# Attention in blocks of 64 tokens on 64x64 tiles of the array: the front of an attention and mixer kernel, before and after

## The chip, the cores and the metric

The kernel runs on one core of a Trainium2 chip. The metric is the device time of one execution in microseconds (us). Each kernel was run several times (the kernel before: 698.68 to 700.90 us over all rounds). One execution of each kernel is recorded by the hardware profiler, and the views below are of that execution; its time can differ by a few tenths of a per cent from the median.

Names of engines in the views: PE is TensorE (matrix products), PEld its weight loads, DVE is VectorE, ACT is ScalarE, POOL is GpSimd, SP is SyncE, which here issues DMA.

Some words: PSUM is the memory that TensorE writes its results to, and a bank is one of its parts. "Tile" has three meanings here: the 128 tokens of one step, a part of TensorE's array that works on a product of its own (as in "four tiles share a round"), and a named buffer (as in "a PSUM tile"). A record is one instruction in the trace; a float32 product of the attention is two matmul records, each with a weight load (the eight products of pkv in a step are 16 records, and the page of the kernel before counts 4194 matmuls and 4194 loads). A round is one start on each of the tiles of the array in use.

## The reference

Part one is attention with decay, in blocks of 64 tokens, with a running 64x64 state for each batch and head. Part two is a token mixer of low rank followed by a channel MLP.

```python
# q, k, v: (4, 8, 768, 64) float32; lam: (8,)
for b in range(nb):                       # 12 blocks of 64 tokens
    sl = slice(b * block, (b + 1) * block)
    qb, kb, vb = (q[:, :, sl], k[:, :, sl], v[:, :, sl])
    intra = np.einsum('bhic,bhjc->bhij', qb, kb) * Dmask[None]
    intra = np.einsum('bhij,bhjd->bhid', intra, vb)
    inter = np.einsum('bhid,bhde->bhie', qb * lam_pow[None], kv_state)
    out[:, :, sl] = intra + inter
    rev_pow = lam[:, None, None] ** (block - 1 - pos[None, :, None])
    kb_dec = kb * rev_pow[None]
    kv_state = lam_block[None, :, None, None] * kv_state + np.einsum('bhsd,bhse->bhde', kb_dec, vb)
...
# x = out as (4, 768, 512); U (768, 32), V (32, 768)
h = x.transpose(0, 2, 1) @ U @ V
u = x + h.transpose(0, 2, 1)
ch = np.maximum(u @ w_ch1, 0.0) @ w_ch2   # 512 -> 2048 -> 512, the weights come as float64
return (u + ch).astype(np.float32)
```

## The kernel before

The kernel first runs the attention (the "front"), and then the two big products of the MLP, which take about 540 us and which the change does not touch. The front goes over 24 tiles of 128 tokens, six for each batch, and one such tile is called a step below. The kernel before treats a tile as one block of 128 tokens. A pair of heads shares the 128 partitions (P = 128, D = 64, HP = 4 pairs, CT = 4).

```python
def prep(s):                                   # q and k with the head dimension on partitions
    ...
    for name, dst in (("q", qt), ("k", kt)):
        pt = bank([P, n, P], "p" + name, "b2") # a PSUM bank each for q and for k
        for a in range(a0, a0 + n):
            nc.tensor.transpose(out=pt[:, a - a0, :], in_=raw[s, name][:, 2 * a : 2 * a + 2, :],
                                identity=ident)
        nc.scalar.copy(dst[:, a0 : a0 + n, :], pt)

def scores(s):                                 # two row tiles, 64x128
    pss = [bank([P, HP, P], "pss", "a1") for x in range(2)]
    for a in range(HP):
        for x in range(2):
            rows = slice(x * D, (x + 1) * D)
            nc.tensor.matmul(out=pss[x][:, a, :], lhsT=kt[rows, a, :], rhs=qt[rows, a, :],
                             start=True, stop=True)
    ...                                        # sm = pss * mask, VectorE

def outputs(s):                                # two column tiles, 128x64; x comes transposed
    px = bank([P, HP, P], "px", "a2")
    for a in range(HP):
        if c > 0:
            for x in range(2):
                rows = slice(x * D, (x + 1) * D)
                nc.tensor.matmul(out=px[rows, a, :], lhsT=kv[:, a, rows], rhs=qs[:, a, :],
                                 start=True, stop=False)
        for x in range(2):
            nc.tensor.matmul(out=px[x * D : (x + 1) * D, a, :], lhsT=vr[:, 2 * a + x, :],
                             rhs=sm[:, x, a, :], start=(c == 0), stop=True)
    nc.scalar.copy(xt, px)
    ...                                        # state(s): pkv products, the state in kv,
                                               # a block-diagonal matrix padded with zeros

def back(s):                                   # x back to tokens on partitions
    for ct in range(CT):
        nc.tensor.transpose(out=px[:, ct, :], in_=xt[:, ct, :], identity=ident)
    nc.scalar.copy(xs[s].rearrange("p (c n) -> p c n", n=P), px)

# one step in program order (cut):
# prep(s+1), turned, scale(s+1), mix, [low at a batch border], outputs(s),
# [low_sum at a border], scores(s+1), back(s), turn
```

In these names `mix` adds the mixer's result to x (product pu), `turn` transposes x for the big products (put), and `turned` is the rest of that splitting on ScalarE and GpSimd. `low` and `low_sum` are the products of low rank, needed once for each batch ("border").

## Time and profile before

| | |
|---|---|
| time, median of 3 | 700.32 us (699.53 to 700.9) |
| front: start to the first matmul of the big products (pz) | 142.2 us |
| the rest | 555.3 us |
| TensorE busy over the span | 98% |
| one steady step of the front | 5.67 us |
| TensorE matmul records in a steady step | 81 |

The prediction below shows the main views of this profile. Two more are needed for the comparison. The first is from the page of the kernel before: the busy tenths of TensorE in 40 equal slices of the span (17.4 us each), and the line of the DMA queue that carries instructions (packets, MB, share).

### The profile page before, as it was taken

Reading aid. Unit: us, or ns where it says so; the run is one execution under the profiler, and the core shown is the slowest. Engines: PE = TensorE matmul, PEld = TensorE weight load, DVE = VectorE, ACT = ScalarE, POOL = GpSimd, SP = SyncE. Lnnn points to the kernel's source line nnn. Section 1 sums busy time; section 2 is a strip of 40 time slices with the busy share of each in tenths; the row PEclk is TensorE's granted clock in tenths of the full one; section 3 lists DMA queues with packets and bytes.
Section 4 is the critical chain, followed back from the end, with each engine's and each line's share of the span. In section 5 each row is a group of like instructions: output and inputs, shape, how many; then the busy total and the mean of one; then the engine's idle time right before and its main releaser. Section 6 shows DMA issues by size and latency. Waiting matters only on the chain.

```text
span 697.5 us, 11418 instructions
## 1 busy us (share of the span) xinstructions
PE 685.6 (98%) x4194; PEld 556.0 (80%) x4194; DVE 502.0 (72%) x905; ACT 306.6 (44%) x543; POOL 108.0 (15%) x91
## 2 busy tenths in 40 slices
PE   7999999998999999999999999999999999999997
PEld 6879797976888888888888888888888888888886
DVE  5768687867899777777779436778577586775864
ACT  4767777844566544444455322232232222322320
POOL 4425554523000000000000000011030030300300
PEclk9999999999999999999999999999999999999999
DMA  9977686224476565556557889966344363352521
GB/s 219 228 182 183 167 221 163 90 81 168 173 256 245 197 210 210 208 209 208 205 206 266 296 304 359 341 206 200 98 153 155 91 211 103 120 185 91 166 92 60
DMA packets 131530, 131.17 MB, mean 188 GB/s; under 512 B 81234, under 2 KB 89426, under 8 KB 131474
## 3 DMA queue, kind: packets, MB, share of 16 engines
q1 hardware_dynamic: 129376, 129.92, 57.8%
q10 hardware_dynamic: 2098, 0.52, 0.3%
q8 instruction: 33, 0.54, 0.3%
q14 instruction: 23, 0.19, 0.1%
HBM read 80.09 MB, written 50.33 MB: 187 GB/s over the span
## 4 chain that ended last, share of the span: by engine, by line
PE 93%; DVE 4%; issue 1%; ACT 1%; DMA 1%; ACTq 0%; DVEq 0%
PE pz L638 25%; PE pz L771 13%; PE pz L769 13%; PE pd L773 13%; PE pd L648 12%; PE pss L341 3%; PE px L364 3%; PE px L359 2%; PE pxn L404 2%; PE pkv L380 2%; PE put L464 1%; PE pk L306 1%; PE pq L306 1%; DVE ut L469 1%; DVE sm L347 1%; PE pr L433 1%
## 5 line engine op out<-in xcount | busy, mean ns | idle before, releaser
L638 PE MATMUL pz<-u_hl,w 128*128 128x512 f32 x768 | 190.6, 398 | 1.1 <-ACT uf L476 1.1
L638 PEld LDWEIGHTS pz<-u_hl,w 128*128 128x128 f32 x768 | 144.4, 188 | 37.1 <-ACT uf L476 1.5
L771 PE MATMUL pz<-w_hl,m 128*128 128x512 f32 x384 | 151.6, 396 | 0.0
L769 PE MATMUL pz<-w_hl,m 128*128 128x512 f32 x384 | 151.6, 396 | 0.0
L773 PE MATMUL pd<-w_d,m 128*128 128x512 f32 x384 | 150.0, 396 | 0.0
L752 ACT ACTIVATE m<-mt 128x512 fp32r<-128x512 f32 x96 | 60.7, 632 | 196.8 <-PE pd L773 137.0
L753 DVE SCALAR_TENSOR_TENSOR m<-rm,m 128x512 fp32r<-128x512 f32 x96 | 71.5, 746 | 52.3 <-ACT m L752 52.1
L653 DVE SCALAR_TENSOR_TENSOR r<-pd,r 128x512 f32<-128x512 f32 x96 | 61.8, 686 | 57.2 <-ACT r L644 47.2
L793 POOL TENSOR_TENSOR o<-o,u 128x512 f32<-128x512 f32 x20 | 29.8, 1522 | 452.1 <-DVE o L791 452.1
L648 PE MATMUL pd<-u_d,w 128*128 128x512 f32 x384 | 98.8, 397 | 0.0
L769 PEld LDWEIGHTS pz<-w_hl,m 128*128 128x128 f32 x384 | 72.3, 188 | 17.7
L771 PEld LDWEIGHTS pz<-w_hl,m 128*128 128x128 f32 x384 | 72.3, 188 | 17.6
L773 PEld LDWEIGHTS pd<-w_d,m 128*128 128x128 f32 x384 | 72.3, 188 | 17.6
L648 PEld LDWEIGHTS pd<-u_d,w 128*128 128x128 f32 x384 | 72.2, 188 | 17.4
L644 ACT ACTIVATE r<-pz 128x512 f32<-128x512 f32 x96 | 51.9, 593 | 62.4 <-PE pz L638 62.4
L754 DVE SCALAR_TENSOR_TENSOR m<-m 128x512 fp32r<-128x512 f32 x96 | 69.1, 721 | 0.9
L751 DVE TENSOR_SCALAR mt<-rm 128x512 uint32<-128x512 uint32 x96 | 46.2, 482 | 28.2 <-DMA rm<-r_d 27.6
L347 DVE TENSOR_TENSOR sm<-pss,mask 128x512 f32<-128x512 f32 x48 | 30.9, 686 | 11.5 <-PE pss L341 9.3
L179 ACT CAST w<-wt 128x512 fp32r<-128x512 f32 x32 | 19.9, 622 | 41.8 <-DVE wt L176 33.5
L364 PE MATMUL px<-sm,vraw 128*64 128x128 f32 x384 | 35.4, 274 | 0.4 <-DVE x_nat L450 0.3
L359 PE MATMUL px<-qs,kv 128*64 128x128 f32 x320 | 32.1, 279 | 0.0
L136 ACT ACTIVATE sc<-sc,ends 128x512 f32<-128x512 uint32 x29 | 21.0, 723 | 19.2 <-DVE sc L132 19.2
(88 smaller groups left out, 761.9 us busy)
## 6 DMA issues: line engine op xcount, KB each, us to landing
r_d<-r SPq DMA_DIRECT2D x96, 256.0 KB, 2.7
rm<-r_d SPq DMA_DIRECT2D x96, 256.0 KB, 2.6
words<-in_moe_w_ch_dram SPq DMA_DIRECT2D x32, 512.0 KB, 4.4
w_d<-w SPq DMA_DIRECT2D x16, 768.0 KB, 3.3
w_hl<-w_d SPq DMA_DIRECT2D x16, 512.0 KB, 6.0
u_d<-x_nat SPq DMA_DIRECT2D x24, 256.0 KB, 3.0
u<-u_d SPq DMA_DIRECT2D x24, 256.0 KB, 4.3
out_dram<-o SPq DMA_DIRECT2D x24, 256.0 KB, 2.0
```

The costliest lines, as they stand in the source:

```text
L364: nc.tensor.matmul(out=px[x * D : (x + 1) * D, a, :], lhsT=vr[:, 2 * a + x, :], rhs=sm[:, x, a, :], start=(c == 0), stop=True,)
L638: nc.tensor.matmul(out=acc[g][0], lhsT=w[:, n, ct, :], rhs=uhl[g][:, n, ct, :], start=(ct == 0 and n == 0), stop=(ct == CT - 1 and n == 1),)
L644: nc.scalar.mul(rs[g], acc[g][0], 1.0 + E)
L648: nc.tensor.matmul(out=acc[g][1], lhsT=w[:, 2, ct, :], rhs=ud[g][:, ct, :], start=(ct == 0), stop=(ct == CT - 1),)
L653: nc.vector.scalar_tensor_tensor(rs[g], acc[g][1], 4096.0, rs[g], ALU.mult, ALU.add)
L751: nc.vector.tensor_scalar(t.bitcast(U32), r.bitcast(U32), HI, None, ALU.bitwise_and)
L752: nc.scalar.activation(out=m[:, 0], in_=t, func=AF.Relu)
L753: nc.vector.scalar_tensor_tensor(m[:, 1], r, 0.0, hi, ALU.max, ALU.subtract)
L754: nc.vector.scalar_tensor_tensor(m[:, 2], hi, E, low, ALU.mult, ALU.subtract)
L769: nc.tensor.matmul(out=pz, lhsT=m[:, 0, cols], rhs=hl[:, 0], start=first, stop=False)
L771: nc.tensor.matmul(out=pz, lhsT=m[:, 1, cols], rhs=hl[:, 1], start=False, stop=end)
L773: nc.tensor.matmul(out=pd, lhsT=m[:, 2, cols], rhs=dd, start=first, stop=end)
```

## The change

The intent: work in blocks of 64 tokens, as the reference does, so that all attention products are 64x64 by 64 columns. The hope is that the array then runs four of them side by side, where before two ran (pairs 7 ns apart in the single records of the trace before). The products come out with tokens on partitions, so the four transposes that turned x back go away, and the state needs no zero blocks. The number of matmul instructions doubles. The diff, cut to its core:

```diff
+    psf = front_ctx.enter_context(tc.tile_pool(name="psf", bufs=1, space=bass.MemoryType.PSUM))
+    def two_banks(name, tag):
+        return psf.tile([P, 2, N], FP32, tag=tag, name=name)
 ...
     def prep(s):
 ...
-            for name, dst in (("q", qt), ("k", kt)):
-                pt = bank([P, n, P], "p" + name, "b2")
+            both = two_banks("pqk", "qk" if a0 == 0 else "px")
+            for i, (name, dst) in enumerate((("q", qt), ("k", kt))):
+                pt = both[:, i, 0 : n * P].rearrange("p (a t) -> p a t", t=P)
 ...
+    def ahead_of(s):              # state products and scores, all on four tiles
+        both = two_banks("psk", "sk")
 ...
+        for a in range(HP):
+            for x in range(2):
+                for t in blocks:
+                    nc.tensor.matmul(out=pkv[half[x], t, a, :], lhsT=ks[half[t], a, x, :],
+                                     rhs=vr[half[t], 2 * a + x, :], start=True, stop=True)
+        for a in range(HP):
+            for t in range(2):
+                for x in range(2):
+                    nc.tensor.matmul(out=pss[half[t], x, a, :], lhsT=kt[half[x], a, half[t]],
+                                     rhs=qt[half[x], a, half[t]], start=True, stop=True)
 ...                               # states kvb (after the first block), kva (after the second)
+    def inter(s):                 # queries x state, four tiles
+        st[s]["px"] = both = two_banks("px", "px")
 ...
+                            out=px[half[t], x, a, :], lhsT=st[s]["qs"][half[x], a, t, :],
+                            rhs=kv[s][half[x], a, :], start=(a == 0), stop=False)
+        st[s]["seen"] = nc.scalar.copy(...)      # one element: orders the two row groups
+    def intra(s):                 # scores x values, two diagonal tiles
 ...
+                        out=px[half[t], x, a, :], lhsT=sm[half[t], x, a, :],
+                        rhs=vr[half[t], 2 * a + x, :], ...)
+        nc.scalar.copy(xs[s].rearrange("p (a x e) -> p x a e", a=HP, x=2), px)
-    def back(s):                  # the four transposes of x: gone
 ...
-        pp = bank([P, C], "pp", "a2" if b < B - 1 else "b2")
+        pp = two_banks("pp", "px")[:, 0] if b < B - 1 else bank([P, C], "pp", "b2")
 ...
-        step = [("prep", s + 1)] * (s + 1 < NS)
+        step = [("prep", s + 1), ("fade", s + 1)] * (s + 1 < NS)
+        step += [("mix", done)] * (done >= 0)
+        step += [("low", b - 1)] * (c == 0 and b > 0)
+        step += [("inter", s)]
         step += [("turned", done - 1)] * (done > 0)
         step += [("scale", s + 1)] * (s + 1 < NS)
         step += [("aside", s)]
-        step += [("mix", done)] * (done >= 0)
-        step += [("low", b - 1)] * (c == 0 and b > 0)
-        step += [("outputs", s)]
+        step += [("ahead_of", s + 1)] * (s + 1 < NS)
         step += [("low_sum", b - 1)] * (c == 0 and b > 0)
-        step += [("scores", s + 1), ("back", s)] * (s + 1 < NS)
+        step += [("intra", s)]
         step += [("turn", done)] * (done >= 0 and done // TG < FG)
```

## The prediction

Item 4's 0.4 us is the author's estimate, and what the trace before shows for it is the pass from one group to the next, 0.15 us from pkv to pss (60.25 to 60.40) and 0.20 from pss to pxn (61.29 to 61.49). The 29 ns of the first rival are half of the 58 ns from pair to pair in pkv. The 0.2 us for "seen", the copy of one element in the diff, is an estimate too: ScalarE's copies of 256 and 512 columns took 0.37 and 0.59 us in the trace before, which would leave some 0.15 for a very short one.

> **What bounds the kernel now.** I read first the page's list of engines and the chain that ended last. TensorE is busy 98% and is 93% of the chain, so the time is the length of TensorE's stream.
>
> ```profile
> PE 685.6 (98%) x4194; PEld 556.0 (80%) x4194; DVE 502.0 (72%) x905; ACT 306.6 (44%) x543; POOL 108.0 (15%) x91
> PE 93%; DVE 4%; issue 1%; ACT 1%; DMA 1%; ACTq 0%; DVEq 0%
> ```
>
> The change touches only the attention front, so next I cut the span into stretches. The timeline shows the first matmul of the two big products (pz) at 142.2 us and the last block transpose at 167.8 us.
>
> ```profile
> core 0: us, PE busy (x) PEld busy (x) DVE busy (x) ACT busy (x) POOL busy (x), PEclk, DMA share, GB/s
> 0.00:142.20 142.20, 136.89 (x1831) 117.31 (x1832) 104.66 (x229) 101.40 (x194) 66.86 (x63) 1.00 0.72 178
> 142.20:170.70 28.50, 25.73 (x135) 18.63 (x133) 20.17 (x34) 14.71 (x26) 10.03 (x8) 1.00 0.35 127
> 170.70:697.50 526.80, 522.94 (x2231) 420.09 (x2231) 377.13 (x644) 190.47 (x324) 31.13 (x21) 1.00 0.56 194
> ```
>
> The front is 142.2 us, and TensorE is its bound too (136.9 us busy; the rest is mostly the first 7 us). The last 526.8 us can't change: same matmuls, 99% busy. Third, the timeline of TensorE for one repeating step (54.11 to 59.78, 59.78 to 65.46: 5.67 us each, one tile of 128 tokens); the columns are start, duration, engine, line, operation and count. Durations overlap, so I read differences of starts.
>
> ```profile
> 59.79 0.69 PE L380 MATMUL pkv<-vraw,ks 128*64 128x64 f32 x16
> 60.40 1.16 PE L341 MATMUL pss<-qt,kt 64*128 64x128 f32 x16
> 61.49 0.66 PE L404 MATMUL pxn<-ident,xt 128*128 128x128 f32 x4
> 61.98 0.60 PE L464 MATMUL put<-ident,x_nat 128*128 128x128 f32 x4
> 62.42 0.60 PE L306 MATMUL pq<-ident,qraw 128*128 128x128 f32 x4
> 62.86 0.60 PE L306 MATMUL pk<-ident,kraw 128*128 128x128 f32 x4
> 63.21 0.48 PE L447 MATMUL pu<-vp 128*128 128x512 f32 x1
> 63.62 0.44 PE L359 MATMUL px<-qs,kv 128*64 128x128 f32 x4
> ...
> 65.46 0.34 PE L380 MATMUL pkv<-vraw,ks 128*64 128x64 f32 x4
> ```
>
> Costs from starts: pkv 0.61, pss 1.09, pxn 0.49, put 0.44, q and k 0.79, pu 0.41, px 1.84 (32 records: state part and score part); sum 5.67 us. Every fp32 product is two records. In the single records pkv goes in pairs, one on each column half, 7 ns apart, a pair every 58 ns; pss in pairs (two row halves) every 111 ns; px in pairs every 109 ns; a transpose takes 109 ns. Passing from one group to the next costs 0.15 to 0.2 us. So now two tiles of the array run together, never four.
>
> The same table for the step from 59.78 to 65.45 gives the other engines: VectorE 4.63 us, ScalarE 4.21, DMA share 0.74 (4.2 us). They are not far behind TensorE's 5.67.
>
> [...]
>
> **The change part by part** (one steady step).
> 1. Products. Four kinds, each 16 matmuls of 64x64 by 64 columns = 32 records: state x queries, keys x values, scores, scores x values. That is 128 records, where there were 64. The first three go round four different tiles: if four tiles share the 58 ns round, 8 rounds x 58 = 0.47 us each, 1.40 in all. The last uses only the two diagonal tiles: 16 rounds x 58 = 0.93. Sum 2.33 us, against pkv + pss + px = 3.54. Four records in 58 ns is 15 ns each; two stand 7 ns apart now, so four fit.
> 2. Removed: 4 transposes (pxn), 0.49 us; x comes out with tokens on partitions.
> 3. Unchanged: q, k transposes 8 x 0.109 = 0.87, put 0.44, pu 0.41.
> 4. [...]small waits between groups; I take 0.4 us.
> Sum for TensorE: 2.33 + 0.87 + 0.44 + 0.41 + 0.4 = **4.45 us**, in place of 5.67.
> 5. VectorE: one mask product of 512 fewer (0.65), one sum of 128x256 more (0.35 to 0.42): 4.63 - 0.28 = **4.35 us**. The four 64-wide updates stay.
> 6. ScalarE: xt copy (0.59) and two kv copies (0.83) go; four 64-wide scalings (my estimate 0.7 us, from the 0.53 us step of a 512-wide activation) and "seen" (0.2) come: 4.21 - 0.5 = **3.7 us**.
> 7. GpSimd: the same multiplications (1.3 + 1.07 + 1.28 us), **3.7 us**.
> 8. DMA: the same bytes in less time. The packet records have 73,728 packets of 256 bytes for q, k, v, 18 ns each: 3072 x 18 / 16 engines = 3.46 us for each tile; the u_d store 128 x 85 / 16 = 0.68. **4.1 us**, more where weights are fetched (1.66 us for 512 KB). All of the front's packets take 102.5 us of sixteen engines.
>
> So TensorE stays the bound by a hair, and four engines stand within 20% of it. Small waits won't all hide: I take **4.65 us** for a steady step, a saving of 1.0.
>
> In the first seven steps (no put, no pu; now 4.91 us each) TensorE would need 3.65, but the loads arrive each 3.46 us plus 0.6 for the U, V and w1 words. The page shows DMA at 97% from 20 to 40 us already:
>
> ```profile
> 20.00:40.00 20.00, 19.61 (x292) 17.35 (x292) 13.95 (x32) 14.52 (x30) 8.17 (x7) 1.00 0.97 233
> ```
>
> I take 4.0 us, a saving of 0.9. At batch borders the low-rank products (1.9 us more) stay.
>
> Sum over 24 steps: start 7.3; six steps at 4.0 = 24.0; first border 5.6; three steps after borders 4.9 = 14.7; nine steady at 4.65 = 41.9; two batch ends at 4.4 = 8.8; two later borders at 6.3 = 12.6; the last 3.4. Total 118.3 us against 142.2: 24 us saved. From 142 to 170 us one transpose group and one pu leave (about 1 us), but that stretch has waits on ScalarE copies that may take it back. 700.3 - 25 = 675 us.
>
> **Rivals.**
> - *Four tiles don't share a round*[...]. Then 128 x 29 = 3.7 us for the products, and a step is 5.8: no gain in steady steps, total 695 to 703. Against it: the 7 ns pairs in both column and row form[...].
> - *A half-way rate*, 20 ns for each record: 0.5 us more a step, total 685.
> - *VectorE, ScalarE or the chain between them becomes the bound*: q and k copies, then the scalings, then "seen", then the second half of the last product; in VectorE the state sum waits for the scalings. By my hand layout of a step "seen" comes about when TensorE needs it. If it doesn't, 0.3 us a step, 7 us: 682.
> - *DMA becomes the bound*: 102.5 us of work in a 118 us front[...], with buffers three or four deep. Stalls of 5 us in all are likely in the first third; they are partly in my 4.0.
> - *All better*: steady steps at 4.4 and early ones at 3.8 give 668.
>
> **Range and chances.** Centre 675, 80% range 667 to 689. Only the first rival ends within 2% (above 686.3) for sure, and I give it and bad mixes of the others about 14%. Slower by 2% would need more than 14 us of new waits in 142: 2%. Faster 0.84.
>
> **What would show it.** In the profile after: single records of the score and state products in rounds of four every 58 to 62 ns, the last product in pairs; no pxn; steady steps of 4.5 to 4.8 us; the first pz matmul near 118 us; DMA share over 0.85 in the front, and TensorE idle behind q or k loads in the first 35 us; VectorE near 90% in the steady steps. Wrong, if [...]TensorE waits on ScalarE ("seen", kt) in each step, or if the stretch after the front grows.

## More of the kernel before

```profile
PE   7999999998999999999999999999999999999997
...
q8 instruction: 33, 0.54, 0.3%
```

TensorE is nearly full from the second slice to the last, and 33 packets of 16 KB brought instructions.

## The result, and the profile after

The changed kernel takes **722.49 us** (median of 4, 721.24 to 723.83) against 699.92 us before (median of 4, 699.47 to 700.9), and its result is correct. It is slower by 3.2%: the ratio is 1.0321, with a 95% interval from 1.0297 to 1.0345. Ratios in this document are the mean time of one kernel's runs over the mean of the other's of the same rounds, so they are not quite the ratios of the medians. Executions over 1.5% slower than the fastest of the same kernel are left out of the means.

The page of the changed kernel, in the same parts as before: engines, TensorE in 40 slices of 18 us, the granted clock and the DMA share in the same slices, the instruction queue, and the chain that ended last.

```profile
PE 672.2 (93%) x5634; PEld 538.2 (75%) x5634; DVE 498.4 (69%) x918; ACT 299.8 (42%) x583; POOL 114.4 (16%) x98
...
PE   6768876789899999999999999999999999999997
...
PEclk9999999998999999999999999999999999999999
...
DMA  9956765411547666555656699985335353353421
...
q8 instruction: 44, 0.72, 0.4%
...
PE 87%; issue 5%; POOL 3%; DVE 2%; ACT 2%; DMA 1%; SPq 0%; ACTq 0%; POOLq 0%; DVEq 0%
```

TensorE has less to do (672.2 us busy, 13.4 less than before) although its matmul records went from 4194 to 5634. But it is no longer full: its first nine slices are at 6 to 8 tenths, where before all but the first were at 9. In the chain, "issue" has grown from 1% to 5%; that is time in which TensorE waited for nothing that the profile shows. The instruction queue carried 44 packets in place of 33: TensorE's matmul records and weight loads together (2 x 5634 and 2 x 4194) are 44.0 and 32.8 times 256. The loads of data are not the main cause: the DMA share falls to 0.5 to 0.7 in the third to seventh slice, and TensorE's waits for DMA in the front add up to 4.8 us, 2.0 of them at the start.

The busy time by stretch, cut as in the prediction (columns as there); the first pz matmul is now at 164.3 us and the last block transpose at 191.7:

```profile
0.00:164.30 164.30, 122.10 (x3274) 98.42 (x3274) 102.62 (x245) 95.36 (x235) 74.28 (x70) 0.95 0.63 157
164.30:191.70 27.40, 25.73 (x125) 18.80 (x125) 16.95 (x26) 11.96 (x22) 8.09 (x7) 0.93 0.26 97
191.70:721.40 529.70, 524.34 (x2239) 420.94 (x2236) 378.84 (x647) 192.43 (x328) 32.05 (x22) 1.00 0.57 194
```

The front is 22.1 us longer (164.3 against 142.2), although TensorE is busy 14.8 us less in it (122.1 against 136.9). The rest is 557.1 us against 555.3. So the loss is idle time in the front: 42 us idle, where before there were 5. The granted clock of the front is 0.95, where before it was 1.00.

Where in the front is it lost? Measured from the scores of one step to the scores of the next, a steady step without an instruction stop (shown below) takes 5.0 to 5.9 us, about as long as before (5.67) and longer than the 4.65 predicted; one with a stop takes up to 7.0. The three border steps and the steps after them take 52.3 us in place of 39.8, so they hold 12.5 of the 22.1 us.

Now TensorE's timeline for one steady step of the changed kernel (columns as in the prediction; in brackets the idle time before a group and what ended it):

```profile
69.57 0.65 PE L387 MATMUL psk<-qt,kt 64*64 64x64 f32 x32
70.04 1.11 PE L436 MATMUL px<-vraw,sm 64*64 64x64 f32 x32
71.08 0.66 PE L505 MATMUL put<-ident,x_nat 128*128 128x128 f32 x4
71.58 0.60 PE L330 MATMUL pqk<-ident,qraw 128*128 128x128 f32 x4
72.91 0.66 PE L330 MATMUL pqk<-ident,kraw 128*128 128x128 f32 x4 [0.73 <-ACT qt L334]
73.32 0.48 PE L488 MATMUL pu<-vp 128*128 128x512 f32 x1
```

The products are about as fast as predicted: the scores take 0.47 us from start to start (69.57 to 70.04; predicted 0.47) and scores x values 1.04 (predicted 0.93). But the transposes of k wait 0.73 us for ScalarE's copy of q. In the kernel before the q and k transposes ran on without a stop. The next view, TensorE's waits in the front (us in total, times, longest us), shows that this happens in every step, and that "issue" comes second:

```profile
PE pqk L330 <- ACT qt L334: 21.0, 23, 2.4
PE px L436 <- issue: 8.3, 5, 2.6
```

A look at single records answers the prediction's main question: do four tiles share a round? These are starts of the state x queries product in the same step:

```profile
68.15 0.22 PE L418 MATMUL px<-kva,qs 64*64 64x64 f32 x1
68.16 0.22 PE L418 MATMUL px<-kvb,qs 64*64 64x64 f32 x1
...
68.21 0.22 PE L418 MATMUL px<-kva,qs 64*64 64x64 f32 x1
```

Four records start within 0.02 us (68.15, 68.16, 68.16, 68.17), and the next round starts at 68.21, about 58 ns later. They do share it. So the 15 ns a record of the prediction are real, in bursts.

An issue stop looks like this in the timeline of the changed kernel. Nothing is waited for, and the product is cut in the middle of its 32 records:

```profile
27.07 0.98 PE L436 MATMUL px<-vraw,sm 64*64 64x64 f32 x26
29.73 0.39 PE L436 MATMUL px<-vraw,sm 64*64 64x64 f32 x6 [1.68 <-issue]
```

Two theories came out of this. **Theory A:** q and k share one PSUM tile of two banks, so k's transposes wait for the copy of q in the other bank; this is the larger part, about 21 us. **Theory B:** the rest are stops in the supply of instructions. A matmul of float32 is two records, each with a weight load, so a steady step has 141 records = 282 TensorE instructions in place of 162. The rival to both was that TensorE, VectorE, ScalarE and GpSimd hold each other in a ring in every step, as the prediction's third rival says, and then taking one wait away would only uncover the next.

### The profile page after: what moved, and what is told of

Its sections match the earlier page's. It is cut to its first block, busy times and chain, and to the rows that moved or that the text cites. A ratio compares the mean times of both kernels' runs of the same rounds, so it can differ in the third digit from the quotient of the medians.

```text
span 721.4 us, 14364 instructions
## 1 busy us (share of the span) xinstructions
PE 672.2 (93%) x5634; PEld 538.2 (75%) x5634; DVE 498.4 (69%) x918; ACT 299.8 (42%) x583; POOL 114.4 (16%) x98
## 4 chain that ended last, share of the span: by engine, by line
PE 87%; issue 5%; POOL 3%; DVE 2%; ACT 2%; DMA 1%; SPq 0%; ACTq 0%; POOLq 0%; DVEq 0%
PE pz L686 24%; PE pz L817 12%; PE pz L819 12%; PE pd L821 12%; PE pd L696 12%; PE px L436 3%; PE pqk L330 2%; POOL qs L353 2%; PE px L418 2%; PE psk L380 1%; PE psk L387 1%; PE put L505 1%; ACT qt L334 1%; POOL ks L342 1%; DMA kraw<-in_k_dram 1%
## 5 line engine op out<-in xcount | busy, mean ns | idle before, releaser
L800 ACT ACTIVATE m<-mt 128x512 fp32r<-128x512 f32 x96 | 60.7, 632 | 195.4 <-PE pd L821 144.1
L330 PE MATMUL pqk<-ident,kraw 128*128 128x128 f32 x96 | 17.6, 308 | 22.9 <-ACT qt L334 21.0
L436 PE MATMUL px<-vraw,sm 64*64 64x64 f32 x768 | 29.0, 222 | 8.3 <-issue 8.3
L436 PEld LDWEIGHTS px<-vraw,sm 64*64 64x64 f32 x768 | 26.1, 138 | 11.2 <-issue 11.2
L353 POOL TENSOR_TENSOR qs<-qt,powq 128x512 f32<-128x512 f32 (+1 forms) x24 | 29.0, 1209 | 29.6 <-ACT qt L334 25.0
```

The costliest lines, as they stand in the source:

```text
L436: mm = nc.tensor.matmul(out=px[half[t], x, a, :], lhsT=sm[half[t], x, a, :], rhs=vr[half[t], 2 * a + x, :], start=(c == 0 and t == 0), sto ...
L800: nc.scalar.activation(out=m[:, 0], in_=t, func=AF.Relu)
```

## The experiments

Eleven kernels ran in twelve runs; the same kernel ran twice as e5_scale_first and e5_again. e4_bench and e11_bench_wide are not in the table: they carry extra work and ran once each (757.92 and 783.35 us). Differences are against the changed kernel where nothing else is said. "Front" is the time of the first pz matmul in the profiled execution.

| run | what it is | median us | ratio to before (95%) | front us |
|---|---|---|---|---|
| before | | 699.92 | 1 | 142.2 |
| after | | 722.49 | 1.0321 (1.0297 to 1.0345) | 164.3 |
| e1_qk_apart | q and k in a PSUM tile each | 701.62 | 1.0036 (1.0019 to 1.0052) | 144.1 |
| e2_border | batch border reordered | 715.86 | 1.0233 (1.0207 to 1.0259) | 158.4 |
| e3_both | e1 and e2 | 701.05 | 1.0025 (1.0002 to 1.0049) | 146.2 |
| e5_scale_first | e1, scalings of q earlier on GpSimd | 700.26 (three fast runs) | 1.0014 (0.9998 to 1.0031) | 142.5 (e5_again) |
| e6_border2 | e5 and the border of e2 | 697.01 | 0.9965 (0.9946 to 0.9983) | 141.3 |
| e7_shift64 | e5 and 64 more instructions at the start | 703.92 | 1.0060 (1.0042 to 1.0077) | 147.7 |
| e9_spread | e6, q transposes moved into the middle | 697.64 | 0.9981 (0.9968 to 0.9995) | 137.9 |
| e10_turn_mid | e6, x transposes moved into the middle | 697.89 | 0.9981 (0.9967 to 0.9994) | 140.1 |
| e12_one_pass | e6 with bf16 in two products (less exact) | 684.59 | 0.9794 (0.9760 to 0.9828) | 126.2 |

### e1_qk_apart: the shared PSUM tile (theory A)

```diff
-            both = two_banks("pqk", "qk" if a0 == 0 else "px")
+            both = None if a0 == 0 else two_banks("pqk", "px")
             for i, (name, dst) in enumerate((("q", qt), ("k", kt))):
-                pt = both[:, i, 0 : n * P].rearrange("p (a t) -> p a t", t=P)
+                if both is None:
+                    pt = one_bank([P, n, P], "p" + name, name + "1")
+                else:
+                    pt = both[:, i, 0 : n * P].rearrange("p (a t) -> p a t", t=P)
```

> The changed kernel with one edit: the transposes of q and k write two one-bank tiles in place of the two halves of one two-bank tile. Theory (a false wait: the k transposes wait for ScalarE's copy of q only because both lie in one tile): the 21 us of waits of the k transposes on the copy of q are gone, each step is 0.7 to 1.0 us shorter, the time is 698 to 706 us. Rival (the front is held by ScalarE or by the instruction stream in any case, and the wait only hides that): less than 6 us gained, 716 us or more, and the wait comes back in another place.

It took 701.62 us: 20.9 us less than the changed kernel by the medians, and the waits that went are 21.0 us. Theory A holds: e1 uses as many PSUM banks, and only the tile is split. That the two numbers agree so closely is partly chance: new waits came in place of the old, and the stretches at half clock (see "The clock" below) shrank from 20.5 to 3.4 us. The same view of waits for this kernel (us in total, times, longest):

```profile
PE px L421 <- POOL qs L356: 6.3, 7, 1.3
PE px L439 <- issue: 4.3, 5, 1.0
```

No wait of k on the copy of q is left in the steady steps. The front is now 144.1 us, still not the 118 of the prediction, and what remains are issue stops and a new wait for GpSimd's scaled queries. GpSimd's timeline shows why that wait exists:

```profile
58.17 1.57 POOL L530 TENSOR_TENSOR u_d<-te,u_hl 128x512 fp32r<-128x512 f32 x1 [4.20 <-ACT te L529]
59.70 1.27 POOL L356 TENSOR_TENSOR qs<-qt,powq 128x512 f32<-128x512 f32 x1
```

Here GpSimd took its work in program order. A part of the x splitting (u_d), which waits for ScalarE, stands ahead of the scaling of q (qs), for which TensorE waits. ScalarE's copy of q was done at 55.51 us (54.93 + 0.58), but GpSimd stood idle 4.20 us until u_d began at 58.17, and began qs at 59.70; TensorE's product then waited 1.06 us for it, until 61.02.

### e2_border and e3_both: the batch border

In the changed kernel the steps around the batch borders are 7.3 to 10.1 us long. There the low-rank product pp takes the PSUM tile of px, and `low_sum` comes late.

```diff
-        pp = two_banks("pp", "px")[:, 0] if b < B - 1 else bank([P, C], "pp", "b2")
+        pp = one_bank([P, C], "pp", "pt") if b < B - 1 else bank([P, C], "pp", "b2")
 ...
         step += [("inter", s)]
+        step += [("low_sum", b - 1)] * (c == 0 and b > 0)
 ...
         step += [("ahead_of", s + 1)] * (s + 1 < NS)
-        step += [("low_sum", b - 1)] * (c == 0 and b > 0)
         step += [("intra", s)]
```

> The changed kernel with another edit, at batch borders alone: the low-rank product gets the bank of the turned tiles in place of the bank of the outputs, and its sum comes before the products of the next tile. Theory (at a border ScalarE, in order, stands behind VectorE's split of the sum, 9 us in all, and the outputs' bank waits for the copy of the low-rank product): 5 to 9 us less, 713 to 718 us; the step after a border falls from about 9 to about 6.5 us. Rival (border steps are long because the clock is halved there): about 722, unchanged.

> Both edits. If the two causes are separate, their gains add: 690 to 700 us. If what is left is bound by the fetching of TensorE's instructions, they add to less, and mid-group gaps of 1 to 2.5 us each 256 TensorE instructions remain, in more steps than before.

Alone (e2) this took 715.86 us, 6.6 us less. The steps right after the borders shrank from 9.18, 7.75 and 8.92 us to 4.94, 6.23 and 6.23, but the border steps themselves grew (10.07 to 13.02 for the last one). On top of e1 (e3) it brought 0.6 us, which is inside the spread of the runs: 701.05 us, above the 690 to 700 that I expected. The two gains don't add. The waits of e2 show one reason:

```profile
PE pqk L330 <- ACT qt L334: 17.0, 23, 1.0
```

The wait on the copy of q is 4.0 us less than in the changed kernel (21.0), and its longest fell from 2.4 to 1.0. So 4.0 of the 6.6 us are part of the wait that e1 removes as a whole. That TensorE, VectorE, ScalarE and GpSimd form a ring, the rival of the two theories, may add to it, but these two runs don't show it. The expectation's other branch, instruction stops, fits too: by the count explained below, under e6 and e7, they are 11.5 us in e3 and 9.8 in e1.

### e5_scale_first and e6_border2: take the ring apart

```diff
         step += [("inter", s)]
-        step += [("turned", done - 1)] * (done > 0)
         step += [("scale", s + 1)] * (s + 1 < NS)
+        step += [("turned", done - 1)] * (done > 0)
```

> The kernel with q and k apart, and in each step GpSimd's multiplications (scaled q of the next tile, scaled k of the one after) ahead of its difference for a turned tile. Theory (what held the steps of the run before was a ring: state product, the copy seen, two ScalarE copies of the turned tile, GpSimd's difference behind them, GpSimd's scaled q behind that, next state product; about 5 us a turn): the 6.3 us of waits of the state products on the scaled q go, 691 to 697 us. Rival (the instruction stops take the time back): 699 to 703, with no waits on the scaled q and longer stops.

> The run with scaled q first once more, since its profile fell on an execution of 1657 us. If the gain of the ring was turned into instruction stops, the waits of state products on scaled q are under 1 us in all, and the stops inside products are longer in all than the 12 us of the run with q and k apart, by 3 to 7 us.

> The run above with the two edits at the batch borders as well. Theory (with the ring gone the border steps show their gain of 2 us each): 686 to 693 us. Rival (as in the run with both edits but the ring: only the places of the instruction stops change): within 2 us of the run above.

e5 took 700.26 us (median of its three fast runs). I leave out the fourth, the profiled execution: it took 1657 us, so I took a second look (e5_again, 699.66 us). I had expected 691 to 697, a miss; its rival (699 to 703, the stops take the time back) came out. The waits (us in total, times, longest) tell why:

```profile
PE px L439 <- issue: 5.6, 4, 2.0
PE px L421 <- issue: 3.4, 3, 1.4
...
PE px L421 <- POOL qs L356: 2.4, 3, 0.8
```

The wait for GpSimd fell from 6.3 to 2.4 us (I had expected under 1), but the issue stops of the two products of x rose from 6.7 us in e1 (4.3, and 2.4 at L421 in the same view) to 9.0. Most of what was saved in one place was spent in the other. e6 took 697.01 us, 0.35% under the kernel before: more than the noise. It is the best version at the full precision; I had expected 686 to 693, a miss. Where its steps have no stop they are as short as predicted. This is a steady step of e6 (TensorE's timeline):

```profile
129.43 0.68 PE L390 MATMUL psk<-qt,kt 64*64 64x64 f32 x32
129.90 1.14 PE L439 MATMUL px<-vraw,sm 64*64 64x64 f32 x32
...
131.46 0.60 PE L333 MATMUL pq<-ident,qraw 128*128 128x128 f32 x4
131.90 0.60 PE L333 MATMUL pk<-ident,kraw 128*128 128x128 f32 x4
```

And this is a step of the same kernel with a stop:

```profile
98.87 0.91 PE L439 MATMUL px<-vraw,sm 64*64 64x64 f32 x22
103.10 0.54 PE L439 MATMUL px<-vraw,sm 64*64 64x64 f32 x10 [3.32 <-issue]
```

Steps without a stop are 4.2 to 4.7 us long; steps with one reach 5 to 9.4. In e6's single records eleven stops of more than 0.25 us stand in the front at the ends of instruction blocks (how these are counted is said under e7): nine inside a product or a group of transposes, 11.8 us, and two between groups, 3.3 us, together 15.1 us of idle time. By the same count the changed kernel has 10.7 us, e1 9.8 and e5_again 14.5.

### e4_bench and e11_bench_wide: the rate of four tiles by itself

To measure the disputed cost apart from the attention, I put 512 + 512 unread float32 matmuls (1024 + 1024 records) at the start of the kernel before: first on four tiles, then on the two diagonal tiles.

```diff
+    halves = [slice(0, D), slice(D, P)]
+    for form in range(2):
+        spare = [bank([P, N], "bench", "a1") for y in range(2)]
+        for i in range(512):
+            t, y = i % 2, (i // 2) % 2 if form == 0 else i % 2
+            nc.tensor.matmul(
+                out=spare[y][halves[t], 0:D], lhsT=ident[halves[y], 0:D],
+                rhs=ident[halves[y], 0:D], start=True, stop=True,
+            )
```

> The kernel before with 512 + 512 extra fp32 matmuls of 64x64 by 64 at its start, nobody reading them: first round all four tiles, then on the two diagonal tiles alone; 1024 records of each, no semaphore waits inside. Theory (TensorE's instructions come in pieces of 16 KB, 256 instructions, a matmul record and its weight load being two; the next piece is asked for too late when records take 15 ns): rounds of four every 58 ns, stopped every 128 matmul records for 0.7 to 2 us, so 1024 records take 20 to 30 us in place of 15; the two-tile part takes 29 ns for each record with shorter stops, 30 to 40 us. Rival (the gaps were other waits): 15 and 30 us, no stops.

e11 is the same with products of 128 columns (`0:P` in the output and the moving operand), so each matmul does twice the work.

> The extra matmuls of the first bench with 128 columns instead of 64, so twice the work with the same number of instructions. Theory (a piece of 256 instructions takes at least about 3.45 us): four-tile records now take 27 ns, a piece 3.5 us, so there are no stops of more than 0.3 us outside the time of dense loads, and the four-tile part takes 27 to 31 us, no more than the 31.4 us it took for half the columns. Rival (a stop of 1.6 us at each border of a piece): eight stops of 1.6 us, 40 us.

On four tiles the 1024 records took 31.4 us (2.55 to 33.98), not the 15 that 58 ns for four would make, and a little over the 20 to 30 that I expected. (For 3.4 us of this part the clock was halved.) On two tiles they took 30.4 us. So with nothing else to do, **four tiles were no faster than two**. The timeline of the four-tile part, once the other loads are quiet:

```profile
22.76 2.09 PE L600 MATMUL bench<-ident 64*64 64x64 f32 x128 [1.36 <-issue]
26.22 2.09 PE L600 MATMUL bench<-ident 64*64 64x64 f32 x128 [1.36 <-issue]
```

A burst of exactly 128 records, then a stop, each 3.46 us. 128 records with their 128 weight loads are 256 instructions. The packets of the instruction queue fit this: each is 16 KB, and in the changed kernel and the kernel before there is one for each 256 matmuls and loads (44 and 33 packets). I take it that one such packet brings 256 instructions, and call these a block. A burst of 128 records lasts some 2 us (2.09), the next block runs only 3.45 us after the one before it began, and the difference is idle (1.36). In the raw records of this stretch, with packets and blocks paired in order, a packet starts about 1.0 us after the block before it began to run, takes 0.9 us, and its instructions run some 1.5 us after it landed.

The wide version shows that the array's work was not the limit. The same four-tile stretch with twice the columns took the same time, 31.2 us (2.55 to 33.80). In the view of TensorE's stretches (columns as before), first e4 and then e11, the busy time goes up by half while the stretch stays:

```profile
2.50:34.00 31.50, 20.75 (x1025) 19.77 (x1025) 2.97 (x10) 1.28 (x1) 2.12 (x2) 0.95 0.36 82
34.10:64.60 30.50, 30.46 (x1027) 30.14 (x1024) 0.00 (x0) 0.00 (x0) 0.00 (x0) 1.00 0.02 4
```

```profile
2.50:33.85 31.35, 30.64 (x1025) 29.46 (x1025) 2.97 (x10) 1.28 (x1) 2.11 (x2) 1.00 0.36 82
```

The rate is 27 ns a record in the quiet stretch (3.45 us / 128 records). That e11 in its quiet stretch also comes to 27 ns can't be told from the array's own time for it, which I estimate at four products of 128 columns every 109 ns (the trace before has a pair of px, 128 columns each, every 109 ns); what counts is that half the columns took as long, with stops. In no run here does a block of 256 follow the one before it in less than 3.45 us. In the kernel before, 81 records in 5.67 us are 70 ns each and its blocks are at least 7.7 us apart, so its supply was never seen. In the changed kernel 141 records in the predicted 4.65 us are 33 ns on average, close to the 27. The products go through at about 15 ns, and I take it that their bursts run into a block that isn't there yet.

### e7_shift64: do the stops belong to the instruction count?

If stops belong to blocks of 256 instructions, then instructions added at the start must leave the stops at the same counts and so move them to other products. This kernel is e5 with 16 unread matmuls = 32 records = 64 instructions ahead of the front.

```diff
+    spare = one_bank([P, N], "spare", "pt")
+    for i in range(16):
+        nc.tensor.matmul(
+            out=spare[half[i % 2], 0:D], lhsT=ident[half[0], 0:D], rhs=ident[half[0], 0:D],
+            start=True, stop=True,
+        )
```

> The run with scaled q first, and 16 fp32 matmuls nobody reads at the start: 64 more TensorE instructions, so all borders between pieces of 256 instructions lie 64 instructions earlier in the work. Theory (stops sit at the borders of pieces): every stop inside a group of products is found 64 instructions earlier in the program, counted in instructions they stay at the same remainder by 256 (194); the time moves by some us either way, because other borders fall among the 64x64 products. Rival (the stops belong to places in the program): they stay at the same products, and the time is the run above plus under 1 us.

In the single records I counted TensorE's instructions (matmuls, weight loads and semaphore instructions) up to each stop inside a product. In the changed kernel and in e1, e5_again and e6 the counts leave the remainder 194 when divided by 256. In e7 they are 706, 962, 1218, 1474, 1730, 3010, 3266, 4034, 4290, 4546 and 4802, again 194 each time, and they now fall into other products (scores as well as scores x values). The program moved by 64 and the stops didn't. This is one of them, in the scores, where e5_again has none:

```profile
43.78 0.35 PE L390 MATMUL psk<-qt,kt 64*64 64x64 f32 x9 [2.40 <-issue]
```

So the stops belong to the place in the instruction stream, and theory B holds. The packets agree: paired with the blocks in order, no block in the fronts of the changed kernel and e6 or in the bench's four-tile part begins less than 1.2 us after its packet landed, and each of the stops at a block's end is over 1.2 to 1.6 us after the landing. The time was 703.92 us, 3.7 us more than e5; those 64 instructions and the other place of the stops share that, and I can't part them.

### e9_spread and e10_turn_mid: spread the slow instructions

A block that mixes fast products with slow transposes (15 ns a record against 109) lasts longer, so moving transposes between the products should let the next block arrive in time. e9 puts the q transposes one tile ahead, between the scores and scores x values; e10 puts the x transposes there. Both are built on e6.

```diff
 e9:      step += [("ahead_of", s + 1)] * (s + 1 < NS)
+         step += [("prep_q", s + 2)] * (s + 2 < NS)
          step += [("intra", s)]
 e10:     step += [("ahead_of", s + 1)] * (s + 1 < NS)
-         step += [("intra", s)]
          step += [("turn", done)] * (done >= 0 and done // TG < FG)
+         step += [("intra", s)]
```

> The best run so far (q and k apart, scaled q first, border edits; 697.0 us, 16 us of stops inside products) with the transposes spread: those of q are done one tile earlier, between the products of the next tile and the last product of this one, those of k stay where they were. Theory (a piece of 256 TensorE instructions can't be had faster than about 3.5 us, more while the loads are dense, so the time a stop takes is what 256 instructions in a row fall short of that): fewer than 8 us of stops inside products, steps without put near 4.2 us, 684 to 691 us[...]. Rival (the stops are a cost for each piece, wherever its border lies): stops stay at 14 to 18 us and the time is 697 to 704.

> The best run so far with the transposes of the turned tile (put) moved from the end of a step to between the products of the next tile and the last product of this one. Theory of the pieces: the first seven steps, which have no put, keep their stops (about 9 us), the later ones lose most of theirs: 690 to 696 us. Rival (cost for each piece): 697 to 701.

They took 697.64 and 697.89 us, the same as e6, where I had expected 684 to 691 and 690 to 696. Both are misses. In e9's profiled execution (694.68 us, its fastest) the stops at the ends of blocks fell from e6's 15.1 to 8.3 us and the front to 137.9, but the times of the other runs don't follow. In e10 the stops before 50 us fell from 8.4 to 6.7 us and the later ones only from 6.7 to 3.6, and new waits of the x transposes on VectorE's sum (2.3 us) took up some of it.

### e12_one_pass: fewer instructions for the same products

Here scaled queries, q, k and the state are bf16, so that the scores and the state x queries products need one record each in place of two (the scores are 16 records in e12's timeline, 32 before). A steady step has 218 instructions in place of 282. The result is less exact; it is not a version to put beside the others.

```diff
-        qt, kt = (att.tile([P, HP, P], FP32, tag=n, bufs=2, name=n) for n in ("qt", "kt"))
+        qt, kt = (att.tile([P, HP, P], BF16, tag=n, bufs=2, name=n) for n in ("qt", "kt"))
 ...      # qs, kva and kvb likewise
```

> A kernel with less exact numbers on purpose (it may fail the comparison): the best run (q and k apart, scaled q first, border edits) with scaled q, q, k for the scores and the state rounded to bf16, so two of the four products take one record for each matmul in place of two. A step has 218 TensorE instructions in place of 282; the other engines have the same instructions. Theory (what keeps that run at 697 in place of 680 is the supply of instructions): stops inside products fall from 16 us to under 6, steps between borders become 4.0 to 4.4 us, the time is 676 to 685 us. Of that, shorter products alone would give up to 0.5 us a step, 12 us, if TensorE's own work were the bound. Rival (the other engines hold the steps by now): 690 us or more, with waits of TensorE on ScalarE, VectorE or GpSimd in place of the stops.

It took 684.59 us, inside the expected range, with the front at 126.2 us and most steady steps at 3.9 to 4.7 us. No stop over 0.1 us falls inside a product at a block's end any more. This fits theory B, but it doesn't measure it: shorter products alone, with 16 + 16 fewer records in a step at 15 ns, are 0.48 us a step or some 11.5 us over 24 steps, an estimate. The stops of e6 (15.1 us) and this estimate together are more than the 15.1 us by which the front shrank (141.3 to 126.2). How much of it is the stops stays open.

## Why the prediction was wrong

By its own numbering:

1. **Products: right.** Four tiles share a round of 58 ns. Scores 0.47, state products 0.5 and scores x values 1.04 to 1.07 us, against 0.47, 0.47 and 0.93. The first rival (no sharing) is refuted for bursts. But my argument against it, pairs 7 ns apart, was one of bursts only. For a long stream the bench shows 27 ns a record, close to the 29 ns at which this rival was reckoned. It had the wrong cause (tiles that don't share a round) and nearly the right number.
2. **Removed transposes and 3., unchanged products: right.** (Its 0.87 us for the q and k transposes is 0.08 more than its own reading of 0.79.) No pxn is left, and the e6 steps without a stop are 4.2 to 4.7 us, around the predicted 4.45 and 4.65.
4. **"Small waits between groups; I take 0.4 us": this is the step that failed.** It was a guess that I filled in without looking at the buffers of the new program. The sum of its terms, 4.45 us, is what a step of e6 without a stop takes, so the other terms were right; what was missing are waits. Two things stood there. First, the wait of k's transposes on the copy of q, 21.0 us over 23 steps or 0.9 us each. It could be read in the diff: one tile `both` takes q in its first bank and k in its second, the copy of q reads the tile before k's transposes write it, and the dependency is kept for the tile, not for the bank (e1, with the same number of banks and a tile for each, has no such wait in its steady steps, and a single one of 0.5 us in the whole front). The prediction named ScalarE waits in each step as a thing that would prove it wrong, but looked for them at "seen" and kt. Second, instruction stops, which were in no term at all: 10.7 us at the ends of blocks in the changed kernel, and 15.1 in e6. The prediction counted 128 records against 64 and priced only their time on the array.
5. to 8. **The other engines: about right, and not the bound.** VectorE's busy time in the front went from 104.7 to 102.6 us, ScalarE's from 101.4 to 95.4 (its four scalings took 1.06 us in a step, not the 0.7 of my estimate), and GpSimd's rose from 66.9 to 74.3 (predicted: the same multiplications). DMA share fell to 0.63, where over 0.85 was forecast. The third rival, the chain between engines, was real but small: 6.3 us of GpSimd waits in e1, and the borders.

The sum: the front was predicted at 118.3 us and came out at 164.3, 46 us more. The experiments give 20.2 of it back with the q and k tiles (e1: 144.1), and 2.8 with the order of GpSimd's work and the border (e6: 141.3). Of the remaining 23, the stops at the ends of blocks in e6's records are 15.1, and the later start (first scores at 8.27 us, where I took 7.3) is 1.0. About 7 us are not accounted for; half clock could be up to 3.4 of them.

**The clock.** In the changed kernel the records show TensorE at half clock in five stretches before 168 us, 20.5 us in all (16.8 in the front), where before there was none until the end; e1 has one of 3.4 us and e6 two. Four of the stretches last 3.41 us and one 6.83. What sets them off isn't shown: TensorE's longest stop in this front is 2.6 us, and in the 3.41 us before each of the five stretches it was busy 30 to 48% of the time (46% in e1, 22 and 10% in e6). No threshold comes out of this, as two other windows of that length with 47 and 48% had no half clock after them. These stretches are why the clock in the front is 0.95. They come after much idle time, and may well be its result, but no run here parts the two. An upper bound, an estimate: if all that ran at half clock had taken half the time, the front would be 8.4 us shorter in the changed kernel (16.8 / 2) and 3.4 in e6 (6.8 / 2).

What stays open: the share of the half clock in the loss, the exact worth of the stops, and why some stops in the front are longer (up to 3.3 us in e6, against 1.4 to 1.6 in the quiet part of the bench). The records narrow it down: the packet isn't slow but late. Before e6's longest stop it took 0.92 us, but started 5.4 us after the block before it began to run, where in the quiet bench it is 1.0 to 1.1. Why it starts late isn't tested.

## What to carry to other kernels

When a change splits products into more and smaller ones, count the instructions as well as the array's time: in these runs a float32 matmul is four TensorE instructions, no block of 256 followed the one before it in less than 3.45 us, so 128 records in a row that would run faster than 27 ns each were held up (e4), whatever the tiles can do; single bursts of 32 records at 15 ns were not. When two results share one multi-bank PSUM tile, check who reads the first half while the second is written; a tile for each cost no more banks here and gave 20.9 us. Take a guess for "small waits" as a sign that the order of the new program still has to be read: here most of the error lay in that term.
